# Mask making moved between stages and loads moved between queues in a fused S4-and-FFN training step

## The chip, the cores and the metric

One core of one Trainium2 chip runs the whole program in one launch. The metric is the device time of one execution in microseconds (us). The kernel before has been timed in three runs: 766.64, 770.0 and 771.95 us, so a median of 770.0 us. One further execution was profiled. The engines are named as the profile names them: PE multiplies matrices, PEld loads PE's weights, DVE and ACT work on vectors, POOL (GpSimd) does small work and can issue transfers, SP issues transfers. Every engine works through its own list of instructions in order, and so does each queue of transfers.

## The reference, cut to what matters

The program computes a forward pass and all its gradients. An S4 convolution layer and a feed-forward network (FFN) share one normalised input; their product is added to the input.

```python
xn = layernorm(A_u)                                  # 2048 x 512
logdA = exp(log_dt)[:, None] * (A_re + 1j * A_im)    # 512 x 128
K = einsum("dn,dnl,dn->dl", C, exp(logdA[:, :, None] * l), dt * B).real
s = irfft(rfft(xn, 2L) * rfft(K, 2L))[:L] + xn * Dskip
o = silu(xn @ w1) @ w2
out = A_u + s * silu(o)
out, vjp = jax.vjp(f, A_u, A_re, A_im, B_re, B_im, C_re, C_im, log_dt, Dskip, w1, w2)
return out, *vjp(grad_out)
```

What the change touches belongs to one part of this: the gradients of A, B, C and log_dt. They need, for each of 512 channels d and 128 states n, a sum over all 2048 positions l of the gradient of K times the powers exp(logdA * l). The kernel has the powers as products of a few tables (X for coarse steps, Y for fine ones), so that sum is done in two small matrix products per group of channels.

## The kernel before, in words

Six stages follow one another in the code, and each engine simply gets its instructions in the order in which the code is written. Where two activities are to overlap, they are written as generators, and a loop takes a step of one and then of another.

**Stage 1** (`stage_1`, L642) runs the forward FFN as a generator `gf` and, beside it, makes the Fourier tables and the powers. A counter `n`, the tick, goes up by one with each step of `gf`; work of the tables is put at fixed ticks, and `last` is the last tick that has any. At tick 28 POOL issues the load XYc (L703). At tick `last + 1` the function `tables_open` (L720) issues, all on POOL, five loads of parts of the table X of the first block and the load TFs of a Fourier table (L744 to L752). The parts of X come from XYd, a buffer in HBM which the stage itself writes by transfers of SP (L509). From tick `last + 2` on, `tables_0` (L762) first takes three copies on ACT, one a tick, and then steps of `chunk_tables` (L788) on DVE; two of these steps (named `prod`, L812 to L816) lie in stage 1, the rest at the start of stage 2. In these ticks DVE also has the products DS (L588, shown by the profile at the helper's line L76). The memory of pools is a stack on each side; a pool that is opened after another has been closed uses the same bytes, and its first writers wait for the last users of these.

**Stage 2** (`stage_2`, L996) starts with two transforms on PE (L991), with the rest of the tables of block 0 on DVE beside them. Then it goes through four blocks b of 128 channels. For each, PE multiplies tables into the convolution kernel K (`chunk_K`, L853) and transposes X and Y (L925, L943) so that stage 5 can load them as XTd and YTd; at the same time DVE makes the tables of block b + 1 (`chunk_tables` again, L799 to L816). `chunk_K` of a block needs the finished X and CY of that block. At the start of this stage POOL loads w2n (L958) and clears DskT (L1007); SP then loads DskT (L1009), the next Fourier table TFs (L638), the X of block 1 (L750) and its XYc (L739). The last of DVE's products DS must be done before the X of block 1 may be loaded.

**Stages 3 and 4** are the remaining transforms, forward and back.

**Stage 5** (`stage_5`, L1598) ends with the part that the change is about. DVE makes masks (`gen_masks`, L178, called at L1657): POOL writes three index tables (L193 to L196) and DVE derives from them MK and Sel. MK picks and weights columns of the gradient Gt, Sel sums groups of partitions. Then come 16 slabs, steps of a generator `Slabs.steps` (L1810). A slab i has

- its loads (`load`, L1733): XTl in two transfers, 64 rows and 18 rows (L1741), and YTl (L1742). XTl has three buffers: slab i + 3 is loaded when PE has done with slab i.
- `Gb` (L1752, two DVE instructions): Gbd, the gradient Gt times the mask MK.
- `P2` (L1764), twice: 16 small products of Gbd and XTl on PE; ACT copies the result to Vb (L1766).
- `D3` (L1775, L1778): DVE multiplies Vb by YTl into T.
- `P3` (L1793): PE sums T over partitions through Sel. After four slabs ACT copies the sum to S_sb (L1796), and `store` (L1798) writes it to HBM as eight transfers of POOL (L1808).

Between these steps PE has other work: the inverse transforms `conv` (L1676, matmuls at L1182) for `ft` 4 to 9 and the gradient of w2 (`w2.run`, L1588), 16 matmuls for each `ft` from 4 to 13. `w2.run` has ACT issue a load AW for `ft + 3` (L1581) and SP store its result (L1595); SP also loads W2T (L1707). At `ft` 9 the first loads of the backward FFN are issued on SP: three hsb (L1856) and two G_s (L1900).

**Stage 6** (`stage_6`, L1940) is the backward FFN and the remaining gradients.

One thing decides the order of transfers that isn't in the code as written. The compiled program has eight counters by which transfers of SP and ACT report that they have landed, and eight for those of POOL. They are given out in turn, so each transfer is issued only when the eighth one before it in its set has landed, whatever it carried.

The lines that set the order around the change, in stage 1 and in the slabs' loads:

```python
if n == last + 1:
    lo.close("bs", "tab", "pr")
    tables_open(k, XY)
if n > last + 1:
    tables_0(k)
...
for p, r in ((slice(0, P, 2), slice(0, 64)), (slice(1, 4 * (NR - 64), 4), slice(64, NR))):
    dma(XT[p].rearrange("p q c n -> p (q c n)"), src[r])
dma(YT[:], k.YTd[i])
```

Of the kernel before, what the change touches and what calls it, by code (L numbers as in the profile page):

```python
# [14 lines left out]
P = 128  # L15
# [162 lines left out]
def gen_masks(k, wk):  # L178

    nc, const = k.nc, k.const  # L180
    cnt = [0]

    def ti(n=1):
        cnt[0] += 1
        return wk.tile([P, n], I32, name=f"mi{cnt[0]}")

    def tf(n=1):
        cnt[0] += 1
        return wk.tile([P, n], F32, name=f"mf{cnt[0]}")
    TSS = nc.vector.tensor_single_scalar  # L190
    TS_ = nc.vector.tensor_scalar
    r = ti()
    nc.gpsimd.iota(r[:], pattern=[[0, 1]], base=0, channel_multiplier=1)  # L193
    loi = ti(16)
    nc.gpsimd.iota(loi[:], pattern=[[8, 16]], base=0, channel_multiplier=0)
    ii = ti(32); nc.gpsimd.iota(ii[:], pattern=[[1, 32]], base=0, channel_multiplier=0)  # L196
    def bit(n):
        b = ti(); TSS(out=b[:], in_=r[:], scalar=n, op=ALU.arith_shift_right)
        TSS(out=b[:], in_=b[:], scalar=1, op=ALU.bitwise_and)
        f = tf(); nc.vector.tensor_copy(out=f[:], in_=b[:])  # L200
        return f
    odd, b1, b2 = bit(0), bit(1), bit(2)
    h = ti(); TSS(out=h[:], in_=r[:], scalar=2, op=ALU.arith_shift_right)
    h8 = ti(); TSS(out=h8[:], in_=r[:], scalar=3, op=ALU.arith_shift_right)
    TSS(out=h8[:], in_=h8[:], scalar=32, op=ALU.add)
    pf = tf(); TSS(out=pf[:], in_=r[:], scalar=4 * (NR - 64), op=ALU.is_lt)

    nb1 = tf(); TS_(out=nb1[:], in0=b1[:], scalar1=-1.0, scalar2=1.0, op0=ALU.mult, op1=ALU.add)
    nc.vector.tensor_tensor(out=pf[:], in0=pf[:], in1=nb1[:], op=ALU.mult)

    def pick(x, y):
        nc.vector.tensor_tensor(out=y[:], in0=y[:], in1=x[:], op=ALU.subtract)
        nc.vector.scalar_tensor_tensor(out=y[:], in0=y[:], scalar=odd[:, 0:1], in1=x[:], op0=ALU.mult, op1=ALU.add)
        return y
    hf = tf(); nc.vector.tensor_copy(out=hf[:], in_=h[:])
    h8f = tf(); nc.vector.tensor_copy(out=h8f[:], in_=h8[:])
    hf = pick(hf, h8f)
    nc.vector.tensor_copy(out=h[:], in_=hf[:])
    one = tf(); TSS(out=one[:], in_=odd[:], scalar=-1.0, op=ALU.is_ge)
    live = pick(one, pf)  # L220
    par = pick(b1, b2)
    m1 = tf(); nc.vector.tensor_tensor(out=m1[:], in0=live[:], in1=par[:], op=ALU.mult)
    m0 = tf(); nc.vector.tensor_tensor(out=m0[:], in0=live[:], in1=m1[:], op=ALU.subtract)
    hi = tf()

    for h0, bits, base, step in ((0, 1, 0, 1), (16, 1, 256, 2), (24, 2, 512, 4), (32, 3, 1024, 1024)):
        a = ti(); TSS(out=a[:], in_=h[:], scalar=(1 << bits) - 1, op=ALU.bitwise_and)
        b = ti(); TSS(out=b[:], in_=h[:], scalar=bits, op=ALU.arith_shift_right)
        af = tf(); nc.vector.tensor_copy(out=af[:], in_=a[:])
        bf = tf(); nc.vector.tensor_copy(out=bf[:], in_=b[:])  # L230
        TS_(out=bf[:], in0=bf[:], scalar1=float(step), scalar2=float(base - step * (h0 >> bits)), op0=ALU.mult, op1=ALU.add)
        nc.vector.scalar_tensor_tensor(out=af[:] if h0 else hi[:], in0=af[:], scalar=128.0, in1=bf[:], op0=ALU.mult, op1=ALU.add)
        if h0:
            m = tf(); TSS(out=m[:], in_=hf[:], scalar=float(h0), op=ALU.is_ge)
            nc.vector.tensor_tensor(out=af[:], in0=af[:], in1=hi[:], op=ALU.subtract)
            nc.vector.scalar_tensor_tensor(out=hi[:], in0=af[:], scalar=m[:, 0:1], in1=hi[:], op0=ALU.mult, op1=ALU.add)
    yield
    lv = tf(16)
    nc.vector.tensor_copy(out=lv[:], in_=loi[:])
    TS_(out=lv[:], in0=lv[:], scalar1=hi[:, 0:1], scalar2=None, op0=ALU.add)  # L240
    MK = const.tile([P, 2, 16, 2], F32, name="MK")
    for e2, msk in ((0, m0), (1, m1)):
        nc.vector.tensor_copy(out=MK[:, 0, :, e2], in_=msk[:].to_broadcast([P, 16]))
        TS_(out=MK[:, 1, :, e2], in0=lv[:], scalar1=msk[:, 0:1], scalar2=None, op0=ALU.mult)
    k.MK = MK

    c = ti(); TSS(out=c[:], in_=r[:], scalar=5, op=ALU.arith_shift_right)
    cf = tf(); nc.vector.tensor_copy(out=cf[:], in_=c[:])
    nc.vector.scalar_tensor_tensor(out=cf[:], in0=odd[:], scalar=8.0, in1=cf[:], op0=ALU.mult, op1=ALU.add)
    iif = tf(32); nc.vector.tensor_copy(out=iif[:], in_=ii[:])  # L250
    k.Sel = const.tile([P, 2, 2, 32], BF16, name="Sel"); k.nSel = const.tile([P, 2, 2, 32], BF16, name="nSel")
    for u in range(2):
        for s in range(2):
            c2 = tf()
            TS_(out=c2[:], in0=cf[:], scalar1=float(16 * u + 4 * s), scalar2=None, op0=ALU.add)
            TS_(out=k.Sel[:, u, s], in0=iif[:], scalar1=c2[:, 0:1], scalar2=None, op0=ALU.is_equal)
    TS_(out=k.nSel[:], in0=k.Sel[:], scalar1=-1.0, scalar2=None, op0=ALU.mult)
    yield
# [383 lines left out]
def stage_1(k):  # L642
# [54 lines left out]
    while True:  # L697
        tick[0] = n
        for fn, a in at.pop(n, ()):
            fn(*a)  # L700
        if n == 28:
            XY = fs.tile([P, 11, 2, 64, 2], BF16, name="XYc", tag="aT")
            nc.gpsimd.dma_start(XY[:].rearrange("p i c q e -> p i (c q e)"), k.XYd[:, 17:NT, 0])  # L703
        if n == last + 1:
            lo.close("bs", "tab", "pr")
            tables_open(k, XY)
        if n > last + 1:
            tables_0(k)
        if next(gf, k) is k:
            break  # L710
        n += 1
        settle(k)
    settle(k); settle(k)
    for _ in k.gc[0]:
        pass
    assert n > last and not mid and not at, (n, last, mid, at)
    ro.close("fs", "fp")

# [1 line left out]
def tables_open(k, XY):  # L720

    lo = k.left
    k.mm = lo.open("mm")
    sa = lo.open("sa")
    k.tabs, k.gt, k.gc = {}, {}, {}
    k.slot = [(sa, sa), None]
    open_tables(k, 0, k.nc.gpsimd, lambda: ld_tf(k, 0, k.nc.gpsimd))
    open_y(k, 0)
    k.gc[0] = copy_tables(k, 0, XY)
    k.gt[0] = chunk_tables(k, 0)  # L730
    k.nt0 = 0
    k.ko = lo.open("ko"); k.xc = lo.open("xc")
    k.Kout = k.ko.tile([P, NH, P], BF16, name="Kout")


# [862 lines left out]
def stage_5(k):  # L1598
# [55 lines left out]
    for ft in range(3):  # L1654
        for _ in w2.run(ft):
            pass
    for _ in gen_masks(k, dkp):  # L1657
        pass
    lo.close("bk", "sel", "kq", "bk3", "tn", "uxl")
    S = Slabs(k, lo.open("sw"))  # L1660
    S.load(0, nc.gpsimd)
# [27 lines left out]
    for ft in range(4, FT):  # L1689
# [7 lines left out]
        if ft == 9:  # L1697
            B = k.B = Bwd(k, fw, k.W2T, DXC)
            for n in range(3):
                B.ld_h(n)  # L1700
            B.ld_g(0); B.ld_g(1)
        if ft == 7:
            nc.scalar.activation(out=k.dtb4[:], in_=ldt[:], func=ACT.Exp)
        if ft == 11:
# [7 lines left out]
class Slabs:  # L1712
# [20 lines left out]
    def load(self, i, q=None):  # L1733
        k, nc = self.k, self.k.nc
        dma = (q or nc.sync).dma_start
        YT = self.YT[i] = self.sw.tile([P, 2, 4, P], BF16, name="YTl", tag="YT", bufs=4)
        XT = self.XT[i] = self.xt[i % 3]
        b, _, _, q0 = slab(i)
        src = k.XTd[b].rearrange("(r q) c n -> r (q c n)", q=64)[:, 256 * q0:256 * (q0 + 16)]
        for p, r in ((slice(0, P, 2), slice(0, 64)), (slice(1, 4 * (NR - 64), 4), slice(64, NR))):  # L1740
            dma(XT[p].rearrange("p q c n -> p (q c n)"), src[r])  # L1741
        dma(YT[:], k.YTd[i])  # L1742

    def Gb(self, i):
        k, nc = self.k, self.k.nc
# [52 lines left out]
    def store(self, b):  # L1798
        k, nc = self.k, self.k.nc
        S_sb = self.S_sb.pop(b)  # L1800
        for ri in range(2):
            for g2 in range(2):
                for u in range(2):
                    z = 32 * (2 * ri + g2) + 16 * u

                    p0 = 16 * (2 * b + u)
                    dst = k.Snd[ri, g2].rearrange("(x p) n -> x p n", p=P)[:, p0:p0 + 16].rearrange("x (w b) n -> x w (b n)", w=4)
                    nc.gpsimd.dma_start(dst, S_sb[z:z + 16])  # L1808

    def steps(self):  # L1810

# [22 lines left out]
class Bwd:  # L1834
# [14 lines left out]
                    nc.tensor.transpose(out=pt[:, d_, t, :], in_=k.DO[:, 4 * tc_ + t, dk * P:(dk + 1) * P], identity=k.ident[:])  # L1849
            (nc.vector.tensor_copy if h else nc.scalar.copy)(out=DOT[:, 2 * h:2 * h + 2], in_=pt[:])  # L1850

    def ld_h(self, n):
        k, nc = self.k, self.k.nc
        tc_, f0 = n // 7, 2 * (n % 7)
        hs = self.hs[n] = self.fw.tile([P, 2, 512], BF16, name="hsb", tag="hsb", bufs=3)
        nc.sync.dma_start(hs[:], k.hTd[tc_][:, f0:f0 + 2])  # L1856

    def dh(self, n):
        k, nc = self.k, self.k.nc
# [35 lines left out]
        self.flush()  # L1895
        self.pend.append((k.dhd[:, 4 * tc_:4 * tc_ + 4, f0 * P:(f0 + 2) * P], dk[:]))

    def ld_g(self, t):
        G = self.G[t] = self.fw.tile([P, D], BF16, name="G_s", tag="G_s")
        self.k.nc.sync.dma_start(G[:], self.k.g_v[:, t, :])  # L1900

    def dx(self, tc_, dhT):

# [139 lines left out]
```

## Time and profile before

| | us |
|---|---|
| median of three runs | 770.0 |
| profiled execution | 771.57 |
| its span in the trace | 769.8 |
| PE busy in the span | 668.3 (87%) |
| DVE busy | 620.0 (81%) |
| ACT busy | 444.7 (58%) |
| POOL busy | 124.3 (16%) |

The span runs from the first to the last instruction; 1.8 us of the execution lie outside it. All times of the trace count from the span's start. Stage 1 ends at about 180 us (PE), stage 2 at about 303, and the slabs of stage 5 run from 490 to 592.6. In a line of the timeline the first number is the start and the second the duration, or, for a group ("x8"), the time from the first to the end of the last; in square brackets stands how long the engine was idle before and what ended that. A line of the waits has the total, the number of waits and the longest. A row of the windows has, for each engine, its busy time, the granted clock of PE as a share of the full one, the busy share of the transfer engines, and the rate.

### The profile page before, as it was taken

What the parts mean: (1) busy time and instruction counts of PE and PEld (TensorE: products, weight loads), DVE (VectorE), ACT (ScalarE), POOL (GpSimd) and SP (SyncE); (2) the same over time, 40 slices, a digit from 0 to 9 for tenths busy, and PEclk for the clock granted to TensorE, in tenths of its full rate; (3) what the DMA queues carried; (4) which work ended last, traced back from release to release, by engine and by line L of the source; (5) the groups of instructions that cost most, each with busy time, mean ns of one, the idle gap of its engine ahead of it and who ended that gap; (6) DMA issues with size and microseconds to landing.
All of it is one profiled execution on the core that took longest, in us unless ns stands there. A gap on an engine that the chain in (4) does not pass through costs nothing.

```text
span 769.8 us, 13823 instructions
## 1 busy us (share of the span) xinstructions
PE 668.3 (87%) x5356; PEld 349.0 (45%) x5356; DVE 620.0 (81%) x965; ACT 444.7 (58%) x541; POOL 124.3 (16%) x185
## 2 busy tenths in 40 slices
PE   4768959796979787999999999899959999898998
PEld 2434535352656665444444444334424554444444
DVE  6799999668999799699999999657555469988820
ACT  4788988974779865565443323245535756664211
POOL 1243171021111003000012120202221000111110
PEclk9998988899989789999999999899999999999999
DMA  9648677889999879998597897679782997878691
GB/s 273 225 151 277 229 252 222 287 260 334 293 312 301 248 194 252 328 377 320 220 339 245 302 355 233 215 233 333 238 298 101 258 244 242 249 225 279 193 338 60
DMA packets 155400, 198.86 MB, mean 258 GB/s; under 512 B 30306, under 2 KB 115945, under 8 KB 149415
## 3 DMA queue, kind: packets, MB, share of 16 engines
q1 hardware_dynamic: 136599, 136.67, 56.7%
q0 software_dynamic: 10800, 46.89, 16.8%
q10 hardware_dynamic: 7936, 14.43, 5.6%
q8 instruction: 42, 0.69, 0.4%
q14 instruction: 23, 0.19, 0.1%
HBM read 112.72 MB, written 83.38 MB: 255 GB/s over the span
## 4 chain that ended last, share of the span: by engine, by line
PE 43%; DMA 10%; ACT 5%; DVE 5%; issue 4%; SPq 1%; POOL 1%; ACTq 0%; DVEq 0%; POOLq 0%
PE ps_f L1158 10%; PE ps_v L1182 8%; PE ps_w L1993 5%; PE ps_w L1588 5%; PE ps_dx L1909 4%; PE ps_da L1870 3%; DMA dhc<-dhd 2%; PE ps_V L1764 2%; DVE dhT L1871 2%; DMA K_b<-Kud 2%; DMA AW<-akd 1%; PE ps_g L1616 1%; DMA XTl<-XTd 1%; PE ps_f L991 1%; DMA co<-od 1%
## 5 line engine op out<-in xcount | busy, mean ns | idle before, releaser
L606 PE MATMUL ps_h<-XNT,W 128*128 128x512 bf16 x224 | 59.7, 415 | 13.4 <-ACT hs L609 13.4
L1182 PEld LDWEIGHTS <-TIs 128*128 128x128 bf16 x384 | 37.3, 98 | 50.8 <-issue 4.3
L579 PE MATMUL ps_o<-W,aT 128*128 128x512 bf16 x224 | 54.9, 394 | 2.5 <-DVE ak L76 2.5
L1588 PE MATMUL ps_w<-DO_all,AW 128*128 128x512 bf16 x224 | 54.4, 393 | 0.0
L1870 PE MATMUL ps_da<-DOT,W2T 128*128 128x512 bf16 x224 | 52.9, 379 | 1.5 <-ACT DOT L1850 1.1
L1909 PE MATMUL ps_dx<-W1T,dhT 128*128 128x512 bf16 x224 | 52.9, 379 | 0.0
L1871 DVE TENSOR_TENSOR dhT<-ps_da,sd 128x1024 bf16<-128x1024 f32 x28 | 34.1, 1222 | 22.0 <-ACT sd L132 16.3
L1766 ACT CAST Vb<-ps_V 128x1024 bf16<-128x1024 f32 x32 | 31.7, 1013 | 34.2 <-PE ps_V L1764 30.2
L1993 PE MATMUL ps_w<-dhc,xn 128*128 128x448 bf16 x256 | 49.3, 352 | 1.6 <-DMA dhc<-dhd 1.6
L1775 DVE TENSOR_TENSOR T<-Vb,YTl 128x2048 bf16<-128x2048 bf16 x16 | 19.6, 1225 | 34.0 <-ACT Vb L1766 32.5
L1158 PEld LDWEIGHTS <-TFs 128*128 128x128 bf16 x312 | 30.1, 98 | 36.9 <-DMA K_b<-Kud 1.8
L927 ACT COPY XT<-pt_xt 128x1024 bf16<-128x1024 bf16 (+1 forms) x44 | 41.5, 1001 | 6.1 <-DMA XTd<-XT 3.2
L1158 PE MATMUL ps_f<-K_b,TFs 128*128 128x512 bf16 x168 | 39.0, 379 | 1.6 <-DMA K_b<-Kud 1.5
L606 PEld LDWEIGHTS <-W 128*128 128x128 bf16 x224 | 22.5, 104 | 38.8 <-issue 21.6
L1918 ACT ACTIVATE dxn<-dxn,c,rstd 128x512 f32<-128x512 f32 x16 | 13.0, 814 | 45.0 <-DVE c L1917 45.0
L991 PE MATMUL ps_f<-xn,TFs 128*128 128x512 bf16 x128 | 31.9, 404 | 6.9 <-DMA TFs<-TFd 6.9
L579 PEld LDWEIGHTS <-aT 128*128 128x128 bf16 x224 | 22.8, 102 | 32.1 <-issue 8.4
L1993 PEld LDWEIGHTS <-xn 128*128 128x128 bf16 x256 | 25.0, 98 | 25.4 <-DMA dhc<-dhd 2.0
L1588 PEld LDWEIGHTS <-AW 128*128 128x128 bf16 x224 | 20.7, 100 | 29.1 <-issue 8.4
L1870 PEld LDWEIGHTS <-W2T 128*128 128x128 bf16 x224 | 21.6, 98 | 26.8 <-issue 2.2
L1894 ACT COPY dhk<-pt_dh 128x1024 bf16<-128x1024 bf16 x28 | 28.0, 1000 | 9.6 <-PE pt_dh L1892 9.6
L925 PE MATMUL pt_xt<-ident_bfloat,X 128*128 128x128 bf16 x328 | 27.3, 237 | 7.2 <-ACT XT L927 5.7
(345 smaller groups left out, 1581.7 us busy)
## 6 DMA issues: line engine op xcount, KB each, us to landing
TIs<-TId SPq DMA_DIRECT2D x24, 512.0 KB, 4.1
XTd<-XT SPq DMA_DIRECT2D x20, 512.0 KB, 6.8
XTl<-XTd SPq DMA_DIRECT2D x15, 512.0 KB, 8.6
hTd<-hs SPq DMA_DIRECT2D x28, 256.0 KB, 2.7
akd<-ak SPq DMA_DIRECT2D x28, 256.0 KB, 2.2
UXl<-UXd POOLq DMA_DIRECT2D x7, 1024.0 KB, 8.2
hsb<-hTd SPq DMA_DIRECT2D x28, 256.0 KB, 5.4
dhd<-dhk SPq DMA_DIRECT2D x28, 256.0 KB, 3.7
```

What stands on the lines that cost most here:

```text
L579: nc.tensor.matmul(out=pso[:], lhsT=aT[:, ft, tt * P:(tt + 1) * P], rhs=W2[:, ft, :], start=(ft == 0), stop=(ft == FT - 1))
L606: nc.tensor.matmul(out=ps[:, j], lhsT=W1[:, dk, ft * P:(ft + 1) * P], rhs=XNT[:, dk], start=(dk == 0), stop=(dk == DK - 1))
L927: nc.scalar.copy(out=XT[:, j0:j0 + len(ks)], in_=pt[:, 0:len(ks)])
L991: nc.tensor.matmul(out=ps[:, c, :], lhsT=TFs[:, t1 + 4 * j, c, :], rhs=src[:, t1 + 4 * j, :], start=(j == 0), stop=(j == 3))
L1158: nc.tensor.matmul(out=ps[:, c, :], lhsT=tab(j), rhs=at(t1 + 4 * j), start=(n == 0), stop=(n == 4 * len(terms) - 1))
L1182: nc.tensor.matmul(out=ps[:, j, :], lhsT=TIs[:, j, 2 * kt + c, :], rhs=B[kt][:, c, (t0 + j) % 4, :], start=(kt == 0 and c == 0), stop=(kt ...
L1588: nc.tensor.matmul(out=ps[:], lhsT=A[:, t, :], rhs=k.DO[:, t, :], start=(t == 0), stop=(t == T - 1))
L1766: nc.scalar.copy(out=self.V[i][:, g2], in_=ps[:].rearrange("p b c n -> p c b n"))
L1870: nc.tensor.matmul(out=ps[:, j], lhsT=self.W2T[:, ft // 2, dk, j * P:(j + 1) * P], rhs=self.DOT[tc_][:, dk], start=(dk == 0), stop=(dk == ...
L1871: nc.vector.tensor_tensor(out=self.dhT[:, f0:f0 + 2, :], in0=ps[:], in1=sd[:], op=ALU.mult)
L1909: nc.tensor.matmul(out=psx[:], lhsT=dhT[:, ft, t % 4 * P:(t % 4 + 1) * P], rhs=self.W1T[:, ft, :], start=(ft == 0), stop=(ft == FT - 1))
L1993: nc.tensor.matmul(out=ps[:], lhsT=k.xn[:, t, dk * P:(dk + 1) * P], rhs=ch[i][:, t, :], start=(t == 0), stop=(t == T - 1))
```

## The change

It has four parts.

1. `gen_masks` is called in the first stage. `tables_open` opens a pool "mk" for its small tiles and makes the generator `k.gm`; more `yield`s cut it into eight steps. From tick `last + 1` on, two steps are taken per tick, after `tables_open` and ahead of `tables_0`. What is left is taken at the end of the stage, and the pool is closed there. The call in stage 5 goes.
2. `Slabs.store` writes the sums of a block in one transfer of POOL, of 128 partitions, instead of eight of 16 partitions. For this the rows of Sel are numbered in another order.
3. In `Slabs.load` the 18-row part of XTl and all of YTl are issued by POOL. The 64-row part stays on SP.
4. The first three hsb and the first two G_s are issued by POOL.

```diff
@@ gen_masks
         return y
+    yield
     hf = tf(); nc.vector.tensor_copy(out=hf[:], in_=h[:])
...
     m0 = tf(); nc.vector.tensor_tensor(out=m0[:], in0=live[:], in1=m1[:], op=ALU.subtract)
+    yield
     hi = tf()
     for h0, bits, base, step in ((0, 1, 0, 1), (16, 1, 256, 2), (24, 2, 512, 4), (32, 3, 1024, 1024)):
...
-    yield
+        yield
     lv = tf(16)
...
-    nc.vector.scalar_tensor_tensor(out=cf[:], in0=odd[:], scalar=8.0, in1=cf[:], op0=ALU.mult, op1=ALU.add)
+    nc.vector.scalar_tensor_tensor(out=cf[:], in0=odd[:], scalar=16.0, in1=cf[:], op0=ALU.mult, op1=ALU.add)
...
-            TS_(out=c2[:], in0=cf[:], scalar1=float(16 * u + 4 * s), scalar2=None, op0=ALU.add)
+            TS_(out=c2[:], in0=cf[:], scalar1=float(4 * u + 8 * s), scalar2=None, op0=ALU.add)
@@ stage_1
             tables_open(k, XY)
+        if n > last:
+            next(k.gm, None); next(k.gm, None)
         if n > last + 1:
             tables_0(k)
...
-    for _ in k.gc[0]:
-        pass
+    for g in (k.gm, k.gc[0]):
+        for _ in g:
+            pass
+    lo.close("mk")
@@ tables_open
     k.ko = lo.open("ko"); k.xc = lo.open("xc")
+    k.gm = gen_masks(k, lo.open("mk"))
@@ stage_5
-    for _ in gen_masks(k, dkp):
-        pass
...
             for n in range(3):
-                B.ld_h(n)
-            B.ld_g(0); B.ld_g(1)
+                B.ld_h(n, nc.gpsimd)
+            B.ld_g(0, nc.gpsimd); B.ld_g(1, nc.gpsimd)
@@ Slabs.load
-        for p, r in ((slice(0, P, 2), slice(0, 64)), (slice(1, 4 * (NR - 64), 4), slice(64, NR))):
-            dma(XT[p].rearrange("p q c n -> p (q c n)"), src[r])
-        dma(YT[:], k.YTd[i])
+        for p, r, d in ((slice(0, P, 2), slice(0, 64), dma), (slice(1, 4 * (NR - 64), 4), slice(64, NR), nc.gpsimd.dma_start)):
+            d(XT[p].rearrange("p q c n -> p (q c n)"), src[r])
+        nc.gpsimd.dma_start(YT[:], k.YTd[i])
@@ Slabs.store
-        for ri in range(2):
-            for g2 in range(2):
-                for u in range(2):
-                    z = 32 * (2 * ri + g2) + 16 * u
-                    p0 = 16 * (2 * b + u)
-                    dst = k.Snd[ri, g2].rearrange("(x p) n -> x p n", p=P)[:, p0:p0 + 16].rearrange("x (w b) n -> x w (b n)", w=4)
-                    nc.gpsimd.dma_start(dst, S_sb[z:z + 16])
+        dst = k.Snd[:].rearrange("r g (x p) n -> (r g x) p n", p=P)[:, 32 * b:32 * b + 32].rearrange("y (v w) n -> y v (w n)", w=4)
+        nc.gpsimd.dma_start(dst, S_sb[:].rearrange("p w n -> p (w n)"))
```

More of the change, by code (lines that the diff above doesn't have):

```diff
@@ L1850, in dot, with ld_h @@
             (nc.vector.tensor_copy if h else nc.scalar.copy)(out=DOT[:, 2 * h:2 * h + 2], in_=pt[:])
-    def ld_h(self, n):
+    def ld_h(self, n, q=None):
         k, nc = self.k, self.k.nc
@@ L1855, in ld_h @@
         hs = self.hs[n] = self.fw.tile([P, 2, 512], BF16, name="hsb", tag="hsb", bufs=3)
[L1856 removed]
+        (q or nc.sync).dma_start(hs[:], k.hTd[tc_][:, f0:f0 + 2])
     def dh(self, n):
@@ L1896, in trans, with ld_g @@
         self.pend.append((k.dhd[:, 4 * tc_:4 * tc_ + 4, f0 * P:(f0 + 2) * P], dk[:]))
-    def ld_g(self, t):
+    def ld_g(self, t, q=None):
         G = self.G[t] = self.fw.tile([P, D], BF16, name="G_s", tag="G_s")
-        self.k.nc.sync.dma_start(G[:], self.k.g_v[:, t, :])
+        (q or self.k.nc.sync).dma_start(G[:], self.k.g_v[:, t, :])
     def dx(self, tc_, dhT):
```

## The prediction

> **What bounds the kernel now.** I read the busy shares of the page first: PE 87%, DVE 81%, so neither bounds the whole span. The windows then tell the stages apart (start of stage 2; block 0; slab 0; the last slabs):
>
> ```profile
> 184.00:201.00 17.00, 11.82 (x63) 4.91 (x65) 16.86 (x27) 5.97 (x7) 1.89 (x4) 0.90 0.93 284
> 201.00:228.00 27.00, 21.09 (x422) 15.64 (x414) 26.83 (x43) 21.87 (x26) 3.68 (x6) 0.96 0.96 304
> 490.00:502.60 12.60, 8.38 (x81) 3.51 (x82) 7.38 (x26) 4.52 (x6) 0.00 (x0) 0.73 0.35 118
> 553.40:592.60 39.20, 28.78 (x333) 13.76 (x330) 23.72 (x32) 16.36 (x19) 6.75 (x13) 0.91 0.67 226
> ```
>
> The third number after the length is DVE. At the start of stage 2 it has no idle time (16.86 of 17.00, 26.83 of 27.00 us): what is put ahead of it there delays it in full. In the last slabs nothing is full: waits set the pace. Which waits, the timeline of the slabs shows:
>
> ```profile
> 481.61 0.15 DVE L198 TENSOR_SCALAR mi<-mi 128x1 int32<-128x1 int32 x1
> 492.52 0.20 DVE L257 TENSOR_SCALAR nSel<-Sel 128x128 bf16<-128x128 bf16 x1
> 493.55 1.05 PE L1764 MATMUL ps_V<-XTl,Gbd 128*32 128x256 bf16 x16 [3.71 <-DVE Gbd L1752]
> ...
> 563.23 5.47 SPq L1900 DMA_DIRECT2D G_s<-in_grad_out_dram  x2
> 569.27 1.26 SPq L1741 DMA_DIRECT2D XTl<-XTd  x2
> 575.63 1.04 PE L1764 MATMUL ps_V<-XTl,Gbd 128*32 128x256 bf16 x16 [6.48 <-DMA XTl<-XTd]
> ```
>
> PE waits 3.71 us for the masks, which hold DVE from 481.61 to 492.72. Later it waits 6.48 us for an XTl that SP issued late, because the issue of G_s ahead of it took 5.47 us. The waits of SP and POOL in 455 to 605 us say why:
>
> ```profile
> SPq L1741 <- DMA AW<-akd: 13.0, 2, 6.6
> SPq L1900 <- DMA AW<-akd: 4.7, 1, 4.7
> POOL Snd L1808 <- ACT S_sb L1796: 94.0, 4, 39.0
> ```
>
> SP stands still until loads AW of ACT have landed, with which XTl and G_s have nothing to do but a shared counter (the eighth transfer before). POOL is nearly empty there. Last, POOL and then DVE where the masks are to go:
>
> ```profile
> 166.88 2.20 POOL L750 DMA_DIRECT2D X<-XYd  x3
> 169.07 0.56 POOL L638 DMA_DIRECT2D TFs<-TFd  x1
> 181.61 0.77 POOL L750 DMA_DIRECT2D X<-XYd  x1 [11.97 <-DMA XYd<-XYg]
> 183.53 0.70 POOL L750 DMA_DIRECT2D X<-XYd  x1 [1.15 <-DVE DS L76]
> 184.23 1.44 POOL L958 DMA_DIRECT2D w2n<-in_B_w_dram  x2
> ```
>
> ```profile
> 168.81 1.22 DVE L518 TENSOR_TENSOR XYg<-ex,b_s 128x1024 bf16<-128x1024 f32 x1
> 173.05 0.69 DVE L76 TENSOR_TENSOR DS<-G,g 128x1024 bf16<-128x1024 bf16 x1 [3.02 <-ACT g L76]
> 176.77 1.09 DVE L812 TENSOR_TENSOR m<-X 128x1792 bf16<-128x1792 bf16 x1 [3.03 <-DMA X<-XYd]
> 193.63 0.29 DVE L816 TENSOR_TENSOR X<-m 128x256 bf16<-128x256 bf16 x1
> 257.64 1.09 DVE L812 TENSOR_TENSOR m<-X 128x1792 bf16<-128x1792 bf16 x1 [5.33 <-DMA X<-XYd]
> ```
>
> DVE has some 6 us idle between 170 and 176.8; from there on it never waits until 252.3. POOL stands still for 11.97 us, until stores of XYd have landed.
>
> **Part 1, the masks in stage 1: +16.8 us.** In before they are 80 DVE instructions in 11.1 us (481.61 to 492.72), each short and each waiting for the one ahead. In stage 1 their first instruction needs an index table of POOL. POOL's three index writes come behind all five loads of X, so not before 184.23 us; they take 0.1 us each, and DVE starts at about 184.4. Until then it stands still from 170.0, since its queue has the masks ahead of the first DS and of the steps of `chunk_tables`. From 184.4 it runs masks (11.1) and the first DS (0.6), and starts the step that began at 176.77 only at 196.15: 19.4 us late. Who waits: `chunk_K` of block 0 needs the X finished at 193.92, now 213.3; PE would be there at 200.8, so it stalls 12.5. Block 1's CY is finished at 225.65 + 19.4 = 245.05; PE, 12.5 late, would need it at 240.7 and is now 16.8 late. Block 2's (247.4 + 19.4 = 266.8) is in time. The X of block 3 can be loaded only when PE has left its buffer, 16.8 late, and by then DVE has used up the 5.33 us it had idle. So 16.8 remains at the end of the stage, and stage 3 waits for this kernel K. In the queues: the memory of the masks' tiles is used next by w2n, whose load on POOL must wait for them, to about 196; DskT behind it on POOL is cleared at 197.7 (185.7 before), so SP loads the next TFs at 199.0 (187.3), and PE's second transform ends at 212.7, just inside the 213.3. SP's loads of X of block 1 wait for the last DS, to about 203; DVE wants them at 228.5. Bounds: nothing, if the masks found the idle 6 us and PE's slack of 6.8 (200.76 less 193.92) hid the rest; 19.4 + 1.4 if PE's slack is worth nothing and its slow start after the stall costs what it did at 192.36, where 32 matmuls took 8.47 us against 7.08. I take 16.8, worked out along the chain, nearer the upper end.
>
> **Parts 1, 3 and 4 in the slabs: -15.0 us.** Without masks Gbd is ready at 483, XTl of slab 0 by 490 (issued at 480.8 and 481.3, landing at most 8.8 later), and PE goes on at 489.84. That is 3.7, and 2.6 of slow matmuls after the gap (8 in 3.53 against 1.83; three `P2` 0.9 longer): 6.3. From 553.4 on PE's waits are 0.9, 2.15, 0.6 and 6.48, and the slow work after the longest costs 1.6: 11.7. Their cause goes: SP issues one transfer for a slab in place of three and none of hsb and G_s, so the eighth transfer before is some 1.6 rounds of `ft` back and no longer the AW of this round. What is late next is DVE: 1.23 + 1.29 + 1.29 = 3.8 a slab, and where no load was late `D3` followed `D3` in 4.34 and 3.92, mean 4.13. Six such from 547.8, and 0.7 for DOT, put the last `D3` at 573.3 against 589.74: 16.4 less. The loads then have 9.4 us for issue (0.7) and landing (median 6.4, longest 8.8): I take off 1.4 for some that come late. Bounds: 3.7, if XTl stays as late as now; 18.0, if all waits go.
>
> POOL's added work: two transfers a slab by 0.55 (its XTl took 0.53, YTl 0.57), 1.1 of 4.1 us, and five of hsb and G_s, 2.8 once. On POOL a load waits for PE to leave slab i, as on SP; behind it stands only the store, whose sum is ready one slab earlier. These loads cost nothing while XTl leads by three slabs; without that lead, up to 1.1 a slab, 7 for the last six.
>
> **Part 2: 0.** Eight issues in 4.50 us become one of 0.6, on an engine that waited 94 us there; the bytes stay. From -0.5 to +0.5: it is read only in stage 6.
>
> Stage 6 starts earlier or later as a whole. **Sum:** 771.57 + 16.8 - 15.0 = 773.4 for the profiled execution. That one is 1.6 above the median of the three runs, so 771.8 as a median, taken as 772.
>
> **A rule weighed.** Row: eight issues of POOL at 551.16 took 4.50 us, 0.56 each, with DVE at work beside them (slowest of all 32: 0.618). The Trainium skill, "SBUF — State Buffer", section "SBUF: two separate sides", says that a transfer issued by GpSimd has its descriptors written through a port that some DVE instructions lock, and gives 620 against 3100 ns for one such overlap. By that, an estimate from its figures, each moved load would be 2.5 us later, a slab's pair 5 us, and the sum would end where the second rival below does. The rows of before don't show it for the DVE work of this stage.
>
> **The rivals.**
> - Faster, 0.14: the masks don't hold DVE up. For it: 6 us idle, and tiny instructions. It needs the index writes before about 172; against it stand POOL's order and the 11.97 us wait. Then DVE is 11.7 - 6 = 5.7 late, less than PE's 6.8: cost 0 to 4, about 759.
> - Slower, 0.18: loads by POOL land late. For it: 0.9 MB a slab in 4.1 us in a stage that already moves 226 GB/s, and one queue for all; against it 5.9 us median landing of POOL's stores, as good as SP's. It decides once a pair lands over 3 us later than now, which uses up the lead of 9.4 less 6.4. With 2.2 us a slab lost from 553 on for the last five slabs, 11 of the 15 are gone: about 783.
> - Slower, 0.10: stage 2 loses more than DVE's delay. SP stands till 203 and then has five X, XYc and two TFs to issue; if ACT's copies of XYc (landing near 214) and the slow start of PE add 4 to 8, about 779.
> - The forecast, 0.58: both hold, within 4 of each side: 766 to 777.
>
> **How the numbers follow.** Within 1% (762.3 to 777.7, about what a measurement here can tell from no change): the forecast (0.56 of 0.58), 0.02 of the first rival, 0.04 of the others: 0.62. Faster: 0.12. Slower: 0.17 + 0.07 + 0.02 = 0.26. 762 to 782 leaves out most of the first rival and the upper part of the second, under 0.2.
>
> **What would show it.** Right: DVE idle from 170 to 184, L198 behind POOL's fifth load of X, the first L853 at about 213 and its third block near 272; in the slabs no wait of PE for Gbd, no G_s on SP, waits for XTl under 3 us in sum, some 99.5 us from the first matmul of `conv` to the last of `P3` in place of 114.4 (478.2 to 592.6). Wrong: masks that run at 170, or XTl waits near 10 us.

## The result, and the profile after

| | before | after |
|---|---|---|
| median, us | 769.88 (6 runs, 766.64 to 771.95) | 780.16 (6 runs, 774.66 to 784.09) |
| profiled execution, us | 771.57 | 779.79 |
| its span | 769.8 | 778.0 |
| first matmul of `chunk_K` | 200.8 | 213.1 |
| first transform of stage 3 | 301.6 | 318.1 |
| first `conv` | 478.2 | 499.7 |
| last `P3` ends | 592.6 | 601.1 |

The change makes the kernel slower: the ratio after to before is 1.013, with a 95% interval of 1.008 to 1.0179, so 6 to 14 us. The forecast was 772, within a range to 782; the time is inside the range, 8 above the forecast, and outside the 766 to 777 that the prediction set around it; it falls in the part "slower", to which the prediction gave 0.26. A second set of six runs (e8 below) gave 778.35 and a ratio of 1.0109 (1.0076 to 1.0142). Two of the experiments' profiled executions (e5 and e9) were disturbed ones and are not read; where a ratio is given, such executions are left out.

Read from the table, the slabs did give time back: they take 101.4 us (499.7 to 601.1) in place of 114.4. But they start 21.5 us late, where the prediction had 16.8. Line numbers of the kernel after are a few higher: `P2` is L1769, `chunk_K` L860, the loads of X L757, `load`'s XTl L1746.

First the windows of after; from left the length, then busy time (and instructions) of PE, PEld, DVE, ACT and POOL, then the granted clock, the transfer engines' busy share and the rate. The first two rows are those shown of before, the others are the end of the slabs.

```profile
184.00:201.00 17.00, 2.90 (x14) 1.11 (x12) 15.33 (x88) 2.52 (x3) 2.29 (x7) 0.69 0.18 57
201.00:228.00 27.00, 21.96 (x393) 14.47 (x396) 26.69 (x41) 16.49 (x18) 1.86 (x3) 0.88 0.77 244
562.00:579.50 17.50, 17.18 (x213) 8.11 (x213) 14.97 (x21) 10.95 (x14) 7.49 (x14) 1.00 0.90 312
579.50:584.00 4.50, 0.35 (x12) 0.21 (x12) 3.01 (x5) 0.78 (x2) 1.63 (x3) 0.89 1.03 314
584.00:601.10 17.10, 16.42 (x175) 7.97 (x170) 9.18 (x12) 8.04 (x9) 0.00 (x0) 0.83 0.28 96
```

At the start of stage 2 PE has 2.90 us of work in 17 (before: 11.82), while DVE is nearly as busy as before (15.33 against 16.86), now with 88 instructions: the masks. Near the end of the slabs PE is full (17.18 of 17.50), then stands still for 4 us while the transfer engines are at 1.03 of their time, and then those are nearly idle (0.28).

The timeline of after where the masks went:

```profile
168.87 1.22 DVE L520 TENSOR_TENSOR XYg<-ex,b_s 128x1024 bf16<-128x1024 f32 x1
183.56 0.70 POOL L757 DMA_DIRECT2D X<-XYd  x1 [1.10 <-DMA XYd<-XYg]
184.27 0.15 POOL L193 IOTA mi<- 128x1 int32 x1
184.46 0.15 DVE L198 TENSOR_SCALAR mi<-mi 128x1 int32<-128x1 int32 x1 [14.37 <-POOL mi L193]
195.97 0.20 DVE L259 TENSOR_SCALAR nSel<-Sel 128x128 bf16<-128x128 bf16 x1
196.08 1.08 DVE L819 TENSOR_TENSOR m<-X 128x1792 bf16<-128x1792 bf16 x1
196.53 1.45 POOL L965 DMA_DIRECT2D w2n<-in_B_w_dram  x2 [11.90 <-DVE nSel L259]
199.57 0.34 SPq L640 DMA_DIRECT2D TFs<-TFd  x1
204.54 8.54 PE L998 MATMUL ps_f<-xn,TFs 128*128 128x512 bf16 x31 [17.64 <-DMA TFs<-TFd]
213.07 1.45 PE L860 MATMUL ps_k<-X,CY 128*32 128x41 bf16 x64
...
244.12 0.24 PE L860 MATMUL ps_k<-X,CY 128*32 128x41 bf16 x4 [1.67 <-DVE CY L811]
244.99 1.25 PE L860 MATMUL ps_k<-X,CY 128*32 128x41 bf16 x60 [0.63 <-DVE CY L813]
```

DVE stands still for 14.37 us behind POOL's index write, which stands behind POOL's fifth load of X; the masks end at 196, the step of `chunk_tables` starts at 196.08, and w2n waits for the masks' memory. PE's 17.64 us of idle time end with the load TFs, which SP issues at 199.57, behind that w2n; the transform that needs it ends at 213.08, and DVE finishes X at 213.22. So two paths from the end of the masks lead to the first `chunk_K` and are equally long. In block 1 it is DVE's CY that PE waits for (1.67 and 0.63 us).

The timeline of after where PE stops near the end of the slabs, with the loads that it waits for:

```profile
511.32 0.62 PE L1769 MATMUL ps_V<-XTl,Gbd 128*32 128x256 bf16 x16
...
568.83 1.61 POOL L1855 DMA_DIRECT2D hsb<-hTd  x3
570.22 0.46 SPq L1746 DMA_DIRECT2D XTl<-XTd  x1
570.43 0.54 POOL L1899 DMA_DIRECT2D G_s<-in_grad_out_dram  x1
572.65 0.55 POOL L1899 DMA_DIRECT2D G_s<-in_grad_out_dram  x1 [1.68 <-issue]
573.34 0.52 POOL L1746 DMA_DIRECT2D XTl<-XTd  x1
583.79 1.04 PE L1769 MATMUL ps_V<-XTl,Gbd 128*32 128x256 bf16 x16 [4.15 <-issue]
584.77 1.89 PE L1848 MATMUL pt_do<-ident_bfloat,DO_all 128*128 128x128 bf16 x16
```

Slab 0 no longer waits for masks (no bracket at 511.32). The `P2` at 583.79 is that of slab 13. Its idle 4.15 us are put down to "issue", that is to nothing the profile names; but the trace's marks of landed transfers name it. SP issued the 64-row part of this slab's XTl at 570.22, and it landed at 578.48. POOL issued the 18-row part only at 573.34, behind hsb and G_s, and it landed at 583.70, just before the matmul: 10.4 us after its issue, where the median over all slabs is 6.4.

The waits of SP and POOL in 455 to 605 us of after answer to the three lines shown of before:

```profile
SPq L1746 <- PE ps_V L1769: 22.1, 8, 6.4
SPq L1712 <- DMA AW<-akd: 8.7, 1, 8.7
POOL XTl L1746 <- PE ps_V L1769: 47.6, 10, 6.6
```

SP's loads of XTl no longer wait for AW at all. They wait for PE to free the buffer, which is what a load in advance should do. What is left of the waits for AW is 8.7 us at a load of W2T and 2.6 us at a store of `w2.run` (L1602).

One more wait is new, in a stage that the change doesn't touch. The timeline of after in stage 3:

```profile
329.41 13.43 SPq L1276 DMA_DIRECT2D XTd<-XT  x4
342.02 1.01 ACT L934 COPY XT<-pt_xt 128x1024 bf16<-128x1024 bf16 x1 [8.56 <-DMA XTd<-XT]
342.93 1.02 ACT L1167 CAST BY<-ps_f 128x1024 bf16<-128x1024 f32 x1
344.00 3.57 PE L1165 MATMUL ps_f<-K_b,TFs 128*128 128x512 bf16 x8 [5.40 <-ACT BY L1167]
```

Four stores XTd, which stage 2 had held back, take SP 13.43 us to issue (before 7.44). ACT waits for their buffer, its copy of BY is behind that, and PE waits 5.40 us and runs slowly for 1.7 more.

### The profile page after: what moved, and what is told of

Read it like the earlier page. It is cut to its first block, busy times and chain, and to the rows that moved or that the text cites. A ratio compares the mean times of both kernels' runs of the same rounds, so it can differ in the third digit from the quotient of the medians.

```text
span 778.0 us, 13723 instructions
## 1 busy us (share of the span) xinstructions
PE 660.9 (85%) x5286; PEld 348.2 (45%) x5356; DVE 619.9 (80%) x965; ACT 444.7 (57%) x541; POOL 127.3 (16%) x192
## 4 chain that ended last, share of the span: by engine, by line
PE 36%; DVE 23%; ACT 9%; DMA 9%; issue 6%; SPq 1%; POOL 0%; ACTq 0%; DVEq 0%; POOLq 0%
PE ps_f L1165 10%; PE ps_v L1189 5%; PE ps_w L1992 5%; PE ps_w L1595 4%; PE ps_dx L1908 3%; PE ps_da L1869 3%; PE ps_V L1769 2%; DMA XYd<-XYg 2%; DMA dhc<-dhd 2%; DMA XTd<-XT 2%; DVE m L821 1%; DVE cm_t L106 1%; DVE cm_t L107 1%; DMA K_b<-Kud 1%; DVE dhT L1870 1%
## 5 line engine op out<-in xcount | busy, mean ns | idle before, releaser
L581 PE MATMUL ps_o<-W,aT 128*128 128x512 bf16 x221 | 52.2, 381 | 2.6 <-DVE ak L76 2.4
L1595 PE MATMUL ps_w<-DO_all,AW 128*128 128x512 bf16 x213 | 50.8, 385 | 1.7 <-issue 1.6
L999 ACT CAST XU<-ps_f 128x1024 bf16<-128x1024 f32 x20 | 20.6, 1028 | 34.4 <-PE ps_f L998 26.7
```

The source lines that it names most:

```text
L581: nc.tensor.matmul(out=pso[:], lhsT=aT[:, ft, tt * P:(tt + 1) * P], rhs=W2[:, ft, :], start=(ft == 0), stop=(ft == FT - 1))
L1595: nc.tensor.matmul(out=ps[:], lhsT=A[:, t, :], rhs=k.DO[:, t, :], start=(t == 0), stop=(t == T - 1))
```

## The experiments

The theory after reading the traces: part 1 costs what was predicted in stage 2; the slabs gain, but the 1 MB of hsb and G_s now meets the loads of the last slabs; and the wait in stage 3 comes on top. Times are medians; each ratio is to runs of the kernel before on the same chip (770.46, 770.23, 769.96 and 769.22 in the four sets).

**e1, parts 2 to 4 alone.** The call of `gen_masks` goes back to stage 5:

```diff
-        if n > last:
-            next(k.gm, None); next(k.gm, None)
@@ stage_5
+    for _ in gen_masks(k, dkp):
+        pass
```

> The changed kernel without part 1: the masks are made in stage 5 again, parts 2, 3 and 4 stay. Theory: part 1 is what costs (some 15 us in stage 2 and a further 7 in stage 3, where PE stood 5.4 us for ACT's BY), and the slabs gain 13, of which some 6 belong to the masks' leaving. Then stages 2 and 3 are as before (first chunk_K at about 201, first conv of BG at about 478), PE waits some 3.7 us for Gbd again, the other waits for XTl go, and the time is about 763. Rival 1: the 7 us of stage 3 come from chance or from another part: conv of BG starts at 483 to 485, time about 769. Rival 2: the slabs' gain came from the masks alone, the moved loads gain nothing: about 770.

765.79 us, ratio 0.9928 (0.9897 to 0.996). The theory holds in direction (it had 763): without part 1 the change is a gain, of 3 to 8 us. Stages 2 and 3 are as before (200.64, 301.29), the slabs take 104.8 us. What PE waits for in them:

```profile
PE ps_V L1766 <- issue: 4.9, 1, 4.9
PE ps_V L1766 <- DVE Gbd L1754: 3.6, 1, 3.6
```

The wait of 3.6 us for Gbd is back. That the other waits for XTl would go did not come true: slab 13's is there without the masks' move.

**e2, part 1 alone** (the kernel before with `gen_masks` in stage 1, as in the change's diff).

> The kernel before with part 1 alone: masks in stage 1, all loads and stores where they were. Theory: it loses all that part 1 costs, 15 in stage 2 and 7 in stage 3, and gains the 6 of the wait for Gbd and the slow matmuls behind it: first conv of BG near 499, time 770 + 21.5 - 6.3 = 785. Rival 1: the stall of 5.4 us in stage 3 belongs to another part or is chance: conv of BG near 493, time about 779. Rival 2: the slabs' 13 us came from the masks' leaving alone: about 778 even with the stall, with no waits for XTl left.

780.98 us, ratio 1.0134 (1.0089 to 1.018). Its profile shows `chunk_K` at 214.24, the first `conv` at 495.80, and no wait in stage 3 but one of 2.3 us for K_b. In the slabs (105.9 us) the late loads are there as before. The waits of PE there, and of SP in 455 to 605 us:

```profile
PE ps_V L1769 <- DMA XTl<-XTd: 10.6, 3, 6.7
```

```profile
SPq L1746 <- DMA AW<-akd: 12.8, 2, 6.7
```

The time lies nearer to rival 1 (779) and the theory is wrong in one thing: up to stage 5 this program's instructions are those of the kernel after, so the wait of 5.40 us in stage 3 is not a fixed cost of part 1.

**e3, index writes early.** POOL's three index writes go ahead of its loads of X, DVE's list stays:

```diff
 def tables_open(k, XY):
+    mask_index(k)      # the three iota, in tiles of k.const
...
-    nc.gpsimd.iota(r[:], pattern=[[0, 1]], base=0, channel_multiplier=1)
...
+    r, loi, ii = k.mi
```

> The changed kernel with POOL's three index writes ahead of its five loads of X and TFs instead of behind them, in tiles of their own that last to the end; DVE's mask instructions stay where they are in its list. Theory: the masks are cheap and only their place behind POOL's loads cost: they then run from about 170, DVE is some 5 to 6 us late instead of 19.4, PE's slack takes most of it, chunk_K starts at 201 to 204, and the stall in stage 3 shrinks or goes: 757 to 762. Rival: the 80 small instructions hold DVE for their own 11 us and more (they can't use the gaps, which lie between the DS and XYg they wait behind): chunk_K at 207 to 210, time 768 to 774.

764.9 us, ratio 0.9924 (0.9897 to 0.9951). The timeline of DVE and POOL, and PE's `chunk_K`:

```profile
167.09 0.37 POOL L182 IOTA mx<- 128x1 int32 x3
170.15 0.14 DVE L201 TENSOR_SCALAR mi<-mx 128x1 int32<-128x1 int32 x1
181.67 0.20 DVE L262 TENSOR_SCALAR nSel<-Sel 128x128 bf16<-128x128 bf16 x1
181.78 1.08 DVE L823 TENSOR_TENSOR m<-X 128x1792 bf16<-128x1792 bf16 x1
184.50 1.42 POOL L969 DMA_DIRECT2D w2n<-in_B_w_dram  x2
200.98 1.32 PE L864 MATMUL ps_k<-X,CY 128*32 128x41 bf16 x64
```

Three instructions of 0.1 us, moved, take 13 to 16 us off the kernel after. The masks run in 170 to 181.9, `chunk_tables` is 5.0 us late (181.78 against 176.77), and PE's slack hides all but 0.2 us of it at the first `chunk_K`. So the cost was in the main the 14.37 us wait ahead of the masks and the loads held up behind them, not the masks' own 11 us. But against e1, which leaves the masks in stage 5, nothing is gained (ratio 0.9924 against 0.9928). By the two profiles the slabs are 3.4 us shorter here (101.4 against 104.8), and the first `conv` is 3.9 later (482.46 against 478.60); e6, with masks in stage 1 as well, has it at 479.68, so why it is late here stays open.

**e4, without part 4.** hsb and G_s on SP again:

```diff
-                B.ld_h(n, nc.gpsimd)
-            B.ld_g(0, nc.gpsimd); B.ld_g(1, nc.gpsimd)
+                B.ld_h(n)
+            B.ld_g(0); B.ld_g(1)
```

> The changed kernel without part 4: the three hsb and two G_s are issued by SP again. Theory: the only long wait of PE left in the slabs (4.15 us at 583.8, for an XTl that POOL and SP issued at 573.3 and 573.8) comes from these five transfers, which stand ahead of it on POOL; without them on POOL it goes, and with two XTl transfers fewer on SP the issue of G_s no longer holds the loads up: 775 to 776. Rival: SP stands still for G_s as before, XTl is late for another reason: a wait of 4 to 8 us stays near that slab, 780 to 784.

778.69 us, ratio 1.0107 (1.0073 to 1.0141): the same as the kernel after, and the theory of this run fell. The wait at slab 13 stays. The windows of e4 there, and PE's wait:

```profile
562.00:579.00 17.00, 16.37 (x210) 7.62 (x208) 15.65 (x22) 10.58 (x13) 4.79 (x9) 1.00 0.91 297
579.00:584.00 5.00, 0.01 (x4) 0.04 (x5) 2.24 (x4) 0.01 (x1) 0.57 (x1) 0.78 1.04 360
```

```profile
PE ps_V L1769 <- DMA XTl<-XTd: 5.6, 1, 5.6
```

Only the part that comes late has changed: here SP issues its XTl of slab 13 at 573.14, behind hsb and G_s, and POOL its own at 569.22; in after it is 570.22 and 573.34 (the 573.8 of the expectation is slab 14's). Whichever queue carries the 1 MB, one part of XTl is issued 3 to 4 us behind the other and lands some 10 us after its issue (583.85 here, 583.70 in after), while the transfer engines are full (1.04 here, 1.03 in after). The Trainium skill, "DMA: Bandwidth & Descriptors", section "Issuing engines are not separate DMA queues", says that transfers started by different engines end up on the same 16 DMA engines, so that spreading them saves only issue time; this run and the kernel after agree, with waits of 5.6 and 4.2 us.

**e5, e3 with hsb and G_s later:**

```diff
         if ft == 9:
             B = k.B = Bwd(k, fw, k.W2T, DXC)
+        if ft == 12:
             for n in range(3):
                 B.ld_h(n, nc.gpsimd)
             B.ld_g(0, nc.gpsimd); B.ld_g(1, nc.gpsimd)
```

> The kernel e3 (index writes early) with the three hsb and two G_s, on POOL as in part 4, issued at ft 12 instead of ft 9, after the loads of the last slabs. In e3 PE waits 5.64 us at 567.8 for the XTl of slab 13, and slower matmuls follow. Theory: these five transfers (1 MB) fill the transfer engines (busy 99 to 103% there) just when the loads of slabs 13 and 14 are wanted, whichever queue they are on; later they fall into a stretch where the transfer engines are nearly idle (5%), 20 us before their first use. The wait goes or falls under 2 us: slabs take 95 to 97 us in place of 101.0, time 764.9 - 5 = 760. Rival: the loads of slabs 13 to 15 and AW saturate the transfers by themselves, since PE frees three buffers within 9 us: the wait stays at 3 to 5 us, 763 to 765.

760.8 us, ratio 0.9857 (0.9826 to 0.9887), 4 below e3: what the theory gave. Whether the wait at slab 13 went in this run is not shown; in e7 and e12 it is.

**e6, masks spread.** Index writes at the very start, one step of the masks a tick, no memory shared with w2n:

```diff
+    mask_index(k)
+    k.gm = gen_masks(k, k.const)
...
+        if n >= 23:
+            next(k.gm, None)
```

> The changed kernel with the index writes at the very start and the eight steps of the masks taken one a tick from tick 23 on, in tiles that share no memory with w2n (scratch tiles share names so that they fit). Theory: made piecewise where DVE had 7 to 9 us idle in each 20 us (140 to 180), the masks cost nothing at all: chunk_K at 200.8, K_b as before, conv of BG at 478 to 480, time 761 to 764, 1 to 3 below e3. Rival: DVE between 140 and 170 feeds PE and ACT with transposes' copies (ak) and products, and each step of 1.5 us delays these: stage 1 ends 2 to 5 us later and the time is 765 to 768, no better than e3.

765.7 us, ratio 0.9929 (0.9902 to 0.9956). The trace agrees with the theory (`chunk_K` at 200.78, K_b at 300.81: stage 2 loses nothing) but the time with the rival: no better than e3. The wait of slab 13 is there (5.7).

**e7, e6 and the later hsb and G_s together.**

> Both of the last two edits: masks spread over the ticks, and hsb and G_s at ft 12. Theory: gains add, 764.9 - 5 - 2 = 757 to 759. Rival (neither edit does anything): 765.

757.29 us, ratio 0.9827 (0.98 to 0.9854): 13 us faster than the kernel before, 21 to 23 than the kernel after, the best version here. The timeline of POOL, and PE's waits in the slabs (which take 96.4 us):

```profile
562.42 0.51 POOL L1750 DMA_DIRECT2D XTl<-XTd  x1 [2.48 <-PE ps_V L1773]
568.35 1.61 POOL L1859 DMA_DIRECT2D hsb<-hTd  x3
569.95 1.06 POOL L1903 DMA_DIRECT2D G_s<-in_grad_out_dram  x2
```

```profile
PE ps_V L1773 <- DMA XTl<-XTd: 3.1, 1, 3.1
```

POOL's last XTl goes out at 562.42, ahead of the 1 MB; the one wait that is left (3.1) is at slab 3.

**e8, the kernel after once more.**

> The changed kernel itself once more, for its profile: in its first one PE stood 5.40 us in stage 3 (at 344) for ACT's BY, ACT for the held stores XTd of SP, whose four issues took 13.4 us in place of 7.4. The run with masks alone (e2), whose instructions are the same up to stage 5, had no such wait. Theory: the wait is a race between POOL's 4 MB of loads and stores issued from 316 on and these stores, decided by one or two us, and comes in some executions and not in others: it may be gone here, and then the span is 6 to 7 below 778. Rival: it belongs to this kernel and comes back within 1 us of 5.4.

778.35 us, ratio 1.0109 (1.0076 to 1.0142). Its profiled execution took 774.42, with a span of 772.6, and in stage 3 has no wait for BY:

```profile
330.19 7.35 SPq L1276 DMA_DIRECT2D XTd<-XT  x4
337.19 1.01 ACT L934 COPY XT<-pt_xt 128x1024 bf16<-128x1024 bf16 x1 [2.95 <-DMA XTd<-XT]
```

The same four stores take 7.35 us here and 13.43 in the first profile of the very same program. So the wait comes and goes; of the six profiles read of programs with these stages 1 to 4 (after twice, e2, e4, e11, e12) two show it, 5.40 in after and 4.02 in e4. In these two POOL's store DXd of 1 MB was still under way when SP issued the first of the four stores, and landed 2.7 and 2.5 us later (332.07 against 329.41, 330.65 against 328.15). In the other four it had landed before, or did within 0.3 us. This fits the race of which the expectation speaks; no run sets the order of these stores, so it is not shown as the cause.

**e9, the held stores ahead of the load TFs:**

```diff
-        if n == 4:
+        if n == 1:
             k.put = nc.sync.dma_start
```

> The changed kernel with the four held stores XTd of stage 3 issued by SP ahead of its load TFs, which waits for PE, instead of behind it: some 12 us earlier (317 in place of 329). The changed kernel's first profile had PE wait 5.40 us in stage 3 behind these stores, its second none, with spans of 778.0 and 772.6. Theory: the wait is a race and comes in most executions, which is why the changed kernel's medians (780.2 and 778.4) stand 4 to 6 above what its second profile and the sum of the prediction give; with the stores early it can't come, and the median falls to 773 to 775. Rival 1: the wait is rare and the spread of the executions comes from elsewhere: 777 to 780. Rival 2: the early stores take the transfer engines from the loads of K_b and TFs, which PE waits for at the start of stage 3: no gain, 778 to 783.

778.29 us, ratio 1.0095 (1.0061 to 1.0128). The theory fell: the median does not move. Either the wait in stage 3 is not what lifts most executions to 778 and above, or the early stores cost as much elsewhere (rival 2); these runs do not show which.

**e10, the same in e7.**

> The kernel e7 (masks spread, hsb and G_s late; median 757.3) with the same earlier stores. Theory: in e7's profile the four stores took the usual 7.4 us and PE did not wait for them, so there is little to gain: 755 to 757. Rival: early stores collide with K_b's loads: 758 to 761.

759.82 us, ratio 0.9859 (0.9818 to 0.99): no gain, and the rival's time; the intervals of e7 and e10 overlap.

**e11, without part 3.** All loads of the slabs on SP:

```diff
-        for p, r, d in ((slice(0, P, 2), slice(0, 64), dma), (..., nc.gpsimd.dma_start)):
+        for p, r in ((slice(0, P, 2), slice(0, 64)), (slice(1, 4 * (NR - 64), 4), slice(64, NR))):
...
-        nc.gpsimd.dma_start(YT[:], k.YTd[i])
+        dma(YT[:], k.YTd[i])
```

> The changed kernel without part 3: all loads of the slabs are issued by SP again; masks in stage 1, one store a block, hsb and G_s on POOL. Theory: part 3 ends the late loads (from masks alone to all but part 4 the slabs went from 105.5 to 100.8 us), so without it SP still stands behind ACT's AW and the slabs take 104 to 106 us, with waits for XTl of 6 to 10 us in sum: 781 to 784. Rival: it was G_s and hsb on SP that made XTl late, and with these on POOL the small loads may stay on SP: slabs 100 to 102 us, 778 to 780.

777.95 us, ratio 1.0103 (1.0063 to 1.0142): the rival's time. SP still waits for AW at XTl, but PE now waits less for it than in e2. First SP, then PE:

```profile
SPq L1746 <- DMA AW<-akd: 13.0, 2, 7.0
```

```profile
PE ps_V L1769 <- DMA XTl<-XTd: 6.6, 3, 3.0
```

With part 3 alone (e4) or part 4 alone (e11) beside part 1 the slabs take 101.2 and 102.8 us; with neither (e2, which lacks part 2 as well) 105.9; with both 101.4 and 100.2. Either does most of the work; the second adds at most 3 us. These are single profiles: the medians (778.69 and 777.95; 780.98; 780.16 and 778.35) do not tell the versions apart.

**e12, the kernel after with hsb and G_s at ft 12** (the diff of e5, and nothing else).

> The changed kernel with the three hsb and two G_s issued by POOL at ft 12 instead of ft 9, and nothing else: the same edit that took e3 from 764.9 to 760.8 and e6 from 765.7 to 757.3. Theory: what the prediction's sum had too large in the slabs is this burst of 1 MB, which meets the loads of slabs 13 and 14 while the transfer engines are full; without it no wait for XTl of over 2 us is left after 560, the slabs take 95 to 97 us and the median is 772 to 775. Rival: the executions above 775 come from waits in stage 3 and elsewhere that this edit does not touch: slabs shorter, but the median at 776 to 779.

772.91 us over 12 runs, ratio 1.0023 (0.9993 to 1.0054). The theory holds: moving five loads by some 15 us takes 5 to 8 us off the kernel after, and what is left is not to be told from the kernel before. The slabs take 97.7 us, a little over the 95 to 97 expected. PE's waits for XTl there, and the windows of the stretch:

```profile
PE ps_V L1770 <- DMA XTl<-XTd: 3.5, 2, 2.0
```

```profile
570.00:581.00 11.00, 9.84 (x128) 4.45 (x116) 10.86 (x17) 6.60 (x8) 3.17 (x6) 1.00 1.02 347
581.00:595.90 14.90, 14.29 (x176) 6.80 (x176) 10.90 (x15) 7.95 (x9) 3.22 (x6) 1.00 0.57 198
```

The transfer engines are still full in 570 to 581, but without hsb and G_s. Slab 13's last part of XTl lands at 581.17, 2.5 us earlier than in after, PE waits 1.46 for it (the 2.0 is at slab 3), and PE keeps its clock (1.00, where after has 0.83 in its last 17 us). By the profiles the slabs are 2.5 to 3.7 us shorter than in the kernel after; the rest of the 5 to 8 us is not seen in them.

## Why the prediction was right, and where it was wrong

**Part 1 in stage 2, right.** Predicted: DVE idle to 184.4, step at 196.15, `chunk_K` at 213.3, block 1 at 245.05, 16.8 us late at the end of the stage. Measured: 184.46, 196.08, 213.07, 244.99, and stage 3's first steady matmuls 15.0 us later than before in the first profile (322.75 against 307.73) and 15.8 in the second (323.53); over all six profiles with this stage 2 it is 13.8 to 18.4. PE's stall before the first `chunk_K` was a wait for TFs, where the prediction named X: it had both paths, and had them end 0.6 us apart (212.7 and 213.3). No run takes away one of them alone. Part 1 with its share of the slabs was 16.8 - 6.3 = +10.5; alone it measured 0.0134 x 770 = +10.3 (e2). That they agree so well is in part chance: in e2's profile the first `conv` is 17.6 late and the slabs are 8.5 shorter.

**Parts 1, 3 and 4 in the slabs: the loads' term was mis-sized.** The causes named went as said: no wait for Gbd, no G_s on SP, no wait of XTl for AW. The step that failed is "the loads then have 9.4 us for issue (0.7) and landing (median 6.4, longest 8.8): I take off 1.4". Without those 1.4 the sum has slabs of 98.0 us (114.4 - 16.4); measured were 101.4 and 100.2, so late loads cost 3.4 and 2.2. The landing times were taken from a stretch at 226 GB/s. In the changed kernel PE frees the last buffers faster, and the loads of these slabs run together with hsb and G_s: 386 GB/s and a transfer share of 1.01 in 570 to 579.5, where YTl takes 10.3 us to land (median), hsb 10.7 and G_s 10.8. The same holds of "five of hsb and G_s, 2.8 once": that took POOL's time to issue them as hidden, though slab 13's XTl stands behind them (3.1 us after SP's part), and left their 1 MB out. Where the time goes in the first profile: PE's wait of 4.15, and 2.7 of slow work behind it (two `P2` 0.42 each, the transposes 1.89 against 1.07 in e7, the eight matmuls of `w2.run` 2.92 against 1.83, all at a granted clock of 0.64 in the window 584 to 592): 6.9 in all. With the burst moved (e12) the slabs take 97.7, so the rest of this sum was right, and the median falls to 772.9. That this lies beside the prediction's 771.8 is in part chance, as the profiles show (us, against the kernel before):

| | forecast | after, first | after, second (e8) | e12 |
|---|---|---|---|---|
| first `conv` later by | 16.8 | 21.5 | 17.3 | 20.1 |
| slabs shorter by | 15.0 | 13.0 | 14.2 | 16.7 |
| behind the slabs | 0 | -0.3 | -0.2 | -0.4 |
| profiled execution | 773.4 | 779.79 | 774.42 | 774.88 |
| median | 772 | 780.16 | 778.35 | 772.91 |

The first profile is 6.4 us above the forecast: 4.7 of them come ahead of the slabs, 2.0 in them. The second is only 1.0 above it, but it is the fastest of the twelve executions of this kernel, whose median is 779.1. So the mis-sized term is the smaller part of the miss where the miss was seen, and where the other executions lose their time is not known.

The next limit was also misnamed. DVE's pace of 4.13 a slab binds for the last slabs at most (DVE 9.36 and PE 9.34 of 9.50 us in 570 to 579.5); over the slabs as a whole it is PE, with some 90 to 93 us of work (92.7 of 101.4 in after, 91.9 of 97.6 in e12, 89.9 of 96.3 in e7). As an estimate from these rows that is the floor; no run reached it.

**Waits for XTl "under 3 us in sum", wrong:** 4.2 and 5.1 in the two profiles. **Slabs in 99.5 us, nearly:** 101.4 and 100.2.

**Part 2 and POOL's work, not contradicted:** the store is one issue of 0.57 us, nothing waits for it. It was not run alone.

**Stage 3, not foreseen.** "So 16.8 remains at the end of the stage" stopped at stage 2. This was put at nothing without a reason. From stage 3's steady matmuls to the first `conv` the first profile lost 6.5 more, the second 1.5, as e1 did too. I took this for the reason of the high medians; e9 speaks against it. What decides it from run to run is open.

**The rule weighed.** POOL's loads land later than SP's: YTl 6.9 us (median in 511 to 572 of after) against 5.5 in the same stretch of e11. That is 1.4, not the 2.5 that was worked out from the figures of the Trainium skill, "SBUF — State Buffer", section "SBUF: two separate sides", and nothing waited for it; POOL's issues beside DVE's work take 0.52 to 0.56 us as before. The stretch also carries 302 GB/s in after and 280 in e11, so even the 1.4 need not come from DVE. No run here shows that DVE holds a transfer of POOL up.

**The rivals.** Faster: did not come; DVE was held up exactly as argued against it, and e3 shows that the rival's condition (index writes before about 172) was the right one. "Loads by POOL land late", 783: something late did come, and at the place where that rival would show, but on SP's queue as well (e4), so its mechanism is not it. "Stage 2 loses more", 779: its number came, its mechanism did not. It had 4 to 8 us on top of the 16.8; stage 2 lost 13.8 to 16.0 in five profiles and 18.4 in the sixth (e12).

What stays open besides: parts 2 to 4 alone gain 3 to 8 us (e1), and beside part 1 only 1 to 3 by the medians (e2 against after). By profile the two gains in the slabs (9.6 in e1, 8.5 in e2) also add up to more than the 13.0 and 14.2 of both. That both take away part of the same waiting is likely; no run singles it out.

## What to carry to other kernels

Before small work is moved ahead on a busy engine, ask what it reads and behind what that stands in the other engine's list: here three writes of 0.1 us behind loads that waited for stores cost more than the 80 instructions moved, and issuing them earlier (e3) gave all of it back, though no more than leaving the masks where they were (e1). When waits of loads are taken away, price the next ones at the rate of the new, denser stretch, in bytes as well as in issues, and put what isn't urgent behind the urgent loads; which queue issues it mattered little, when it is issued mattered 5 to 8 us (e12, e7).

## What the runs showed of the hardware that was not expected

- The same program's four stores of 0.5 MB took SP 7.35 us to issue in one execution and 13.43 in another, and PE then stood still for 5.40 us in the second only; the twelve runs of the kernel after spread over 774.4 to 784.1.
- With the transfer engines at a share of 1.01 (570 to 579.5 us of after), two loads of 128 KB took 10.8 us to land (median); the wait of 4.15 us for a load of this stretch cost PE another 2.7 at a granted clock of 0.64.
